# Attention, dense MLP and expert MLP: the stores that fill the token table and clear the output wait until the partial sums and all chunks of x have been read back

## The chip, the cores and the metric

One core of a Trainium2 chip runs the whole program in one launch. The metric is the device time of that launch in microseconds; lower is better. The kernel before took 1200.53 us as the median of three runs (1197.09 to 1201.72).

## What is computed

Three layers follow one another. Attention has 4 batches, 8 heads, 576 tokens and heads of 64 columns, with a decay and a causal mask. Its output x (2304 tokens of 512 columns) goes through a dense MLP of 2048 hidden columns, and that output goes through a layer of 8 experts, of which each token takes two:

```python
decay = cum[:, :, :, None] - cum[:, :, None, :]          # cum: running sum of log f
attn = softmax(where(causal, -1e9, scale * q @ k.T + decay)); x = attn @ v
h = x @ w_in;  y = (h * sigmoid(1.702 * h)) @ w_out       # 512 -> 2048 -> 512
noisy = y @ w_gate + log1p(exp(y @ w_noise)) * noise      # 8 experts, the best two of each token
for e in range(8):                                        # w1: 512 -> 1024, w2: 1024 -> 512
    out[mask] += weight[mask] * (maximum(y[mask] @ w1[e], 0) @ w2[e])
```

All is float32. To keep that accuracy on TensorE, every operand is split into a rounded part (names that end in h) and the rest (names that end in l), and each product is three matmuls: high by high, high by low, low by high.

## The kernel before

The work is written as Python generators, "threads". A class `Planner` runs them on a modelled core while the program is built: a thread yields an operation with its engine and a modelled duration, a buffer token, or an event. The planner emits operations in the order of their modelled start times; among those that could start at the same time the one with the lower priority number goes first. The result is a fixed order of instructions for each engine. On the chip every engine works through its own order, and semaphores keep the data dependences.

All plain transfers are issued by SP into one hardware queue that all 16 DMA engines serve. GpSimd issues only the indirect ones. The planner's model of that queue moves bytes at a fixed rate and lets it run 2.1 us ahead (`DEEP`).

The stages are these. Attention writes x to DRAM in two parts, `x2`, unscaled, with the scale of each token in `rd`. The dense MLP takes x in nine chunks of 256 tokens and its 2048 hidden columns in four quarters. Chunks 0 to 5 (`early_c`) get their first quarter between the products of attention (`filler`, line 1025), and the partial sums of those chunks go out to `yp` (line 1050). When attention has ended, its SBUF is given to `yacc`, the sums of all tokens, and to the remaining chunks of x:

- `yload` (line 1126) reads the six partial sums back, line 1128.
- `xin` (line 1117) reads chunks 6 to 8 (`rest`), and then chunks 0 to 3 once more (`back`); 4 and 5 are still in SBUF (`kept`). One chunk takes four loads of x (line 933) and two of its scales (line 938). DVE or POOL adds the two parts and multiplies by the scale (lines 927 and 928), ACT rounds to `xh` (948), and the rest is `xl` (338 or 339). Each needs one of four staging buffers, `stok`.
- `wprep` (line 341) brings a block of 512 rows or columns of the MLP's weights, also by way of a staging buffer (load: 355). ACT and DVE take the 64-bit words apart (365 to 371), ACT rounds (382), the rest is taken by DVE or POOL (338 or 339).

For each chunk and quarter, line 982 makes h, lines 957 to 962 make the gated gh and gl (ACT, DVE, ACT or POOL, DVE or POOL), and line 1002 adds their products into y. The order is the first quarter of chunks 6 to 8, and then three quarters of all nine, `kept + rest + back` in each. In the last quarter each chunk is routed: its tokens are scattered as rows into the token table `tab` in DRAM, 640 rows for each expert (line 1282). Then each expert reads its rows and adds its results into the output with an accumulating scatter (line 1524).

Before the scatters, every place of the table must hold a padding row and the output must be zero. That is `prefill` (line 1071): 40 stores of 258 KB from the tile `padr` into the table (line 1076), and then 23 stores of 256 KB into the output (line 1079), 63 in all. It has priority 10200, behind the weights of the second and third quarters and the chunks. It waits for `a_done`, the end of attention, and issues a store whenever the modelled queue has nothing with a lower number that is ready.

Of the kernel before, what the change touches and what calls it, by code (L numbers as in the profile page):

```python
# [17 lines left out]
DRAM = bass.MemoryType.DRAM  # L18
# [15 lines left out]


class Tokens:
    """Numbered buffers that threads take and give back."""

    def __init__(self, ids):
        self.free = [(0.0, i) for i in ids]  # L40
# [12 lines left out]


class Planner:
    """Runs generators as threads of a modelled core and emits their instructions in the order of
    the modelled start times, so that every engine's queue holds what can start first.

    A thread yields (engine, us, emit), a Tokens (it is sent the number taken), (Tokens, number) to give
    one back, an Event to wait for, ("set", Event), or ("go", generator, priority)."""  # L60

    LAT = {"PE": 0.2, "ACT": 0.14, "DVE": 0.14, "POOL": 0.14, "DMA": 0.9, "SWQ": 2.2}
    DEEP = 2.1
# [111 lines left out]


def ways(kind, *w):
    """Of the ways to do an operation of a kind, those that it may take."""
    return ("any",) + tuple(x for x in w if x[0] in WAYS.get(kind, ("DVE", "ACT", "POOL")))


# [26 lines left out]

@with_exitstack
def tile_attn_mlp_moe(ctx, tc, q, k, v, f, w_in, w_out, gates, noise, w1, w2, out):  # L210
    """q: [pair, (head d), (tokens 512.., 0..511)], k: [head, d, token], v: [pair, p, i, head, d] of the tokens 128 i + p
    (the last 64: any tokens), w_in and w1: [.., block, p, k, n] of the rows 128 k + p and columns 128 block + n,
    gates: [p, k, (gate, noise)], noise: [p, t, e] of the tokens 128 t + p; w_in and w_out: 64-bit words."""
    nc = tc.nc
    B, H, S = f.shape
    D = k.shape[1]
# [17 lines left out]
    P = Planner()  # L234
# [50 lines left out]
    block = c_([128, CAP // 128], "block")  # L285
# [8 lines left out]

    begun = event()

    # ------------------------------------------------------------------ weights
    watok, wbtok = Tokens(range(4)), Tokens(range(4))
    wplace = {i: wpool for i in range(4)}
    stok = Tokens(range(NST))  # L300
# [12 lines left out]
        return splace.get(i, stg).tile(shape, dt, name=name, tag=f"st{i}")  # L313

    class Weight:
        """A [128, 512] block of weights, split, for `uses` users."""

        def __init__(self, uses, late):
            self.ready, self.uses, self.late = event(), uses, late
# [5 lines left out]


    def rounded(dst, src, n, scale=1.0, kind=""):
        """dst = scale * src, rounded to dst's type."""
        w = onec if scale == 1.0 else eighth
        at = src.base_partition()  # L330
        w = w[at:at + src.shape[0]]
        ones = bass.AP(tensor=w.tensor, offset=w.offset, ap=[list(w.ap[0])] + [[0, x] for x in src.shape[1:]])
        return ways(kind, ("DVE", dve(n / 2), lambda: nc.vector.tensor_scalar(dst, src, scale, None, op0=OP.mult)),
                ("ACT", act(n, True), lambda: nc.scalar.activation(dst, src, AF.Copy, scale=scale)),
                ("POOL", pool1(n), lambda: nc.gpsimd.tensor_tensor(dst, src, ones, op=OP.mult)))
# [3 lines left out]
                ("POOL", pool2(n), lambda: nc.gpsimd.tensor_tensor(dst, a, b, op=OP.subtract)))  # L339

    def wprep(src, wt, pool, letter):
        """A DRAM block of [128, 512] -> a rounded part and the rest; `wd`: of 64-bit words."""
        wd = src.dtype != F32
        n = KD * 128
        yield begun
        if wd:
            ahead = yield pre
        else:
            if wt.late:
                yield placed[letter]  # L350
            sl = yield pool
        st = yield stok
        raw = stage(st, [128, n], src.dtype, "wraw")
        dst = raw.rearrange("p (k n) -> p k n", k=KD) if len(src.shape) == 3 else raw
        yield ("DMA", dma(128 * n * (8 if wd else 4)), lambda: nc.sync.dma_start(dst, src))
        val = raw
        if wd:
            pair = raw.bitcast(F32).rearrange("p (n w) -> p n w", w=2)
            low = raw.bitcast(U32).rearrange("p (n w) -> p n w", w=2)[:, :, 0]
            top, val = pair[:, :, 1], pair[:, :, 0]  # L360
            ut = yield utok
            g = stg.tile([128, n], F32, name="wg_", tag=f"wg{ut}")
            u = stg.tile([128, n], U32, name="wu_", tag=f"wu{ut}")
            gi = g.bitcast(U32)
            yield ("ACT", act(n, True), lambda: nc.scalar.activation(g, top, AF.Abs))
            yield ("DVE", dve(n / 2), lambda: nc.vector.tensor_scalar(g, g, TINY, None, op0=OP.max))
            yield ("DVE", dve(n / 2), lambda: nc.vector.tensor_scalar(
                u, gi, 3, 0x3FFFFFFF, op0=OP.logical_shift_left, op1=OP.bitwise_and))
            yield ("DVE", dve(n), lambda: nc.vector.scalar_tensor_tensor(
                u, top.bitcast(U32), 0xC0000000, u, op0=OP.bitwise_and, op1=OP.bitwise_or))  # L370
            yield ("DVE", dve(n), lambda: nc.vector.scalar_tensor_tensor(
                low, low, 29, u, op0=OP.logical_shift_right, op1=OP.bitwise_or))
            yield (utok, ut)
            sl = yield pool
            yield (pre, ahead)
        if not wt.late:
            nplaced[letter] += 1
            if nplaced[letter] == NQ * FPQ:
                yield ("set", placed[letter])
        wt.pool, wt.slot = pool, sl  # L380
        hi, lo = [wplace[sl].tile([128, n], FR, name=f"w{letter}{x}", tag=f"w{letter}{x}{sl}") for x in "hl"]
        yield ("ACT", act(n, True), lambda: nc.scalar.copy(hi, val))  # L382
        yield subtract(lo, val, hi.bitcast(F32), n, "wl")
        yield (stok, st)
        wt.hi, wt.lo = hi, lo
        yield ("set", wt.ready)

    # ------------------------------------------------------------------ attention
    a_done = event()
    xdone = [event() for _ in range(B)]  # L390
    f_done, c_done = event(), event()
# [2 lines left out]
    def attention(actx):  # L394
        raw, ep, one, sm, xo = [actx.enter_context(tc.tile_pool(name=n, bufs=b)) for n, b in
                                (("a_raw", 1), ("a_e", 1), ("a_one", 1), ("a_sm", 5), ("a_x", 1))]
# [50 lines left out]
        def pair(p):  # L447
            b, hp = divmod(p, PPB)
            base = p * 100.0
            sa = sall[b % 2]  # L450
            # loads
            rw = yield raws
            RQ, RK, vt = [raw.tile(sh, F32, name=f"r{n}", tag=f"r{n}{rw}") for n, sh in
                          (("q", [128, S]), ("k", [128, 2, S]), ("v", [128, 5, 2, D]))]
# [108 lines left out]
            if not p:  # L563
                yield ("set", begun)

            # score tiles
            fronts = [event() for _ in range(5)]
            backs = [event() for _ in range(5)]
            PT = {}
# [2 lines left out]
            def tile_(i):  # L572
# [4 lines left out]
                n = (i + 1) * 128  # L577
# [105 lines left out]
                    if not sleft[b]:  # L683
                        yield ("set", sdone[b])
                yield ("go", ended())
                # transposed probabilities
                if i == 0:
                    PT[2] = yield pt01
                    PT[0] = [one.tile([128, 2, 2, 256], FR, name=f"pt01{x}", tag=f"pt01{x}{PT[2]}") for x in "hl"]
# [133 lines left out]
            P.go(shares(b), b * 100.0 * PPB)  # L823
        return one, init

    # ------------------------------------------------------------------ set-up
    def setup(one, init):
        buf = one.tile([B * H, 5, S], F32, name="buf", tag="pt24h0")
        ft, ones, cum = buf[:, 0], buf[:, 1], buf[:, 2]
# [64 lines left out]
    pad_ok = event()  # L894
    setup(*attention(actx))

    # ------------------------------------------------------------------ dense MLP
    ring = Tokens(range(2))
    gtok = Tokens(range(4))
    gplace = {i: gpool for i in range(4)}  # L900
# [116 lines left out]
            wt = W[letter, fi] = Weight(NCH, False)  # L1017
            P.go(wprep(src, wt, pool, letter), WPRIO + fi if fi < FPQ else 10000 + 90 * (fi // FPQ) - 45 + fi % FPQ)

    # chunks that the first batches fill run between the attention's products  # L1020
    NE_ = B - 1
    early_c = [c for c in range(NCH) if (c + 1) * CH <= NE_ * S]
    ypd = {}
# [43 lines left out]
    for i, c in enumerate(early_c):  # L1067
        ypd[c] = event()
        P.go(filler(c, FP0 + FP1 * i, i and reads[i - 1], reads[i]), FP0 + FP1 * i)

    def prefill():
        yield pad_ok
        yield a_done
        for e in range(E):
            for b in range(CAP // 128):
                yield ("DMA", 0.74, lambda: nc.sync.dma_start(tab[e * RS + b * 128:e * RS + (b + 1) * 128, :], padr))
                yield ("wait", -2.5)
        for b in range(out.shape[0] // 128):
            yield ("DMA", 0.73, lambda: nc.sync.dma_start(out[b * 128:(b + 1) * 128, :], padr[:, 0:DM]))
            yield ("wait", -2.5)  # L1080
# [45 lines left out]
    def yload(c):  # L1126
        yield ypd[c]
        yield ("DMA", 1.46, lambda: nc.sync.dma_start(
            yacc[:, 2 * c:2 * c + 2], yp[c * CH:(c + 1) * CH].rearrange("(t p) d -> p t d", p=128)))
        yield ("set", yin[c])  # L1130

    for i, c in enumerate(rest):
        P.go(xin(c), base - 200 + i)
    for i, c in enumerate(back):
# [2 lines left out]
        P.go(xkept(c), base)  # L1137
    for c in early_c:
        P.go(yload(c), base - 100 + c)

    # ------------------------------------------------------------------ routing
    order = {Q: kept + rest + back for Q in range(NQ)}
    order[0] = rest
    FLOOR = NCH - 4
# [216 lines left out]
            after = turns[Q, c]  # L1361
            n += 1

    # ------------------------------------------------------------------ experts
    NB = CAP // 128
    NBE = EARLY // 128
    EE = list(range(NEE))
# [19 lines left out]
    def group(gi_):  # L1387
# [53 lines left out]
            yield z  # L1441
        if small:
            yield (stok, xs_)
        # products
        if gi_:
            yield mm1_end[gi_ - 1]
        halves = [(0, N)] if N <= 512 else [(0, N // 2), (N // 2, N)]
# [49 lines left out]
    def second(gi_, H_, hev, ids, wab, prio, xet):  # L1497
# [39 lines left out]
        def add(j, b):  # L1537
            wt, (hh, hl, _) = W2[gi_, "b", j], H_[j]
            for n, (a, w) in enumerate(((hh, wt.hi), (hh, wt.lo), (hl, wt.hi))):
                nc.tensor.matmul(ye[b][0], a[:, b * 128:(b + 1) * 128], w, start=(j == 0 and n == 0),  # L1540
                                 stop=(j == FB - 1 and n == 2))
        # the last of the parts go block by block, so that the last group's blocks end one after another
        ends = TJ if gi_ == len(groups) - 1 else 1
        for js in [[j] for j in range(FB - ends)] + [list(range(FB - ends, FB))]:
            for j in js:
# [38 lines left out]
    mctx.close()  # L1584
    body.close()

    # ------------------------------------------------------------------ rows past an expert's slots
    most = nc.values_load(nbi[0:1, E:E + 1], min_val=0, max_val=NOV)
    with tc.If(most > 0), ExitStack() as octx:
        one = octx.enter_context(tc.tile_pool(name="o_one", bufs=1))  # L1590
# [49 lines left out]


def lay(I):
    """The arrays as the kernel takes them; no element changes."""
    import numpy as np
    B, H, S, D = I["q"].shape
    NP = B * H // 2
# [40 lines left out]
```

## Time and profile before

| | |
|---|---|
| runs, median of three | 1200.53 us (1197.09 to 1201.72) |
| profiled execution, span from first to last instruction | 1201.4 us |
| profiled execution, its own time | not listed apart from the three runs above |
| instructions | 18895 |
| PE, weight loads beside it | 1128.1 us (94%), 1000.0 us |
| DVE | 751.1 us (63%) |
| ACT | 529.2 us (44%) |
| POOL | 299.4 us (25%) |
| granted TensorE clock, mean | 0.968 |
| DMA | 167.46 MB, mean 139 GB/s |
| stores of `padr` into the table | 40, issued from 304.0 to 397.8 us |
| stores of `padr` into the output | 23, issued from 398.2 to 415.1 us |

Busy time alone says which engine has the most work, and not what it waits for. The timelines give that: an entry ends, in brackets, with the idle time ahead of it and with what ended it. The granted clock is 1.00 where TensorE has its upper level of 2.4 GHz and 0.50 at the lower one, 1.2 GHz; values between are a mix over the stretch.

### The profile page before, as it was taken

To read this page: it belongs to the slowest core of one execution; us is meant where nothing else is said; L and a number is where in the kernel's file an instruction comes from. 1 tells how busy PE (TensorE), PEld (TensorE's weight loads), DVE (VectorE), ACT (ScalarE), POOL (GpSimd) and SP (SyncE) were. 2 spreads that over 40 slices of the span, in tenths; PEclk is the share of its full clock that TensorE was granted. 3 is DMA by queue.
4 is the path that set the end of the run, shared out by engine and by line. 5 is a ranking of instruction groups with operands and counts; after the bars stand their busy time and mean duration, and the time that the engine had idled before them with its cause. 6 is when DMAs were issued, how large, how long until landed. Compare 5 with 4: busy or idle time off the path is not lost.

```text
span 1201.4 us, 18895 instructions
## 1 busy us (share of the span) xinstructions
PE 1128.1 (94%) x6905; PEld 1000.0 (83%) x6905; DVE 751.1 (63%) x1609; ACT 529.2 (44%) x1251; POOL 299.4 (25%) x316
## 2 busy tenths in 40 slices
PE   7998999999897999999999988999999999999993
PEld 6777888887796998998988877889998989899993
DVE  8999999975558747745777875645434343434410
ACT  4687777674353424433333343544333333333311
POOL 4457654410214001000132343112020202020202
PEclk7998899999898999999999988999999999999997
DMA  8668657619999903101021357676363636262503
GB/s 217 185 189 225 167 153 184 171 66 235 278 280 263 361 2 97 44 1 37 15 96 75 117 160 223 189 191 181 83 152 83 153 78 152 77 158 71 115 1 46
DMA packets 92096, 167.46 MB, mean 139 GB/s; under 512 B 9310, under 2 KB 29534, under 8 KB 91994
## 3 DMA queue, kind: packets, MB, share of 16 engines
q1 hardware_dynamic: 83354, 146.17, 43.1%
q0 software_dynamic: 8640, 20.00, 7.9%
q8 instruction: 56, 0.92, 0.3%
q14 instruction: 46, 0.38, 0.1%
HBM read 112.60 MB, written 49.40 MB: 135 GB/s over the span
## 4 chain that ended last, share of the span: by engine, by line
PE 61%; DVE 15%; DMA 12%; issue 5%; ACT 3%; POOL 2%; SPq 1%; another core or an unknown queue 0%; POOLq 0%; DVEq 0%; ACTq 0%
PE h L1483 15%; PE ye L1540 14%; PE y L1002 12%; PE h L982 12%; PE PT L727 2%; PE O L773 2%; DMA out<-yt,ids 2%; DVE kb L338 1%; DMA xl<-rd 1%; DVE qa L338 1%; DMA xh<-x 1%; POOL out L1524 1%; DVE pt24l L445 1%; DMA xrh<-x 1%; DVE m L585 1%
## 5 line engine op out<-in xcount | busy, mean ns | idle before, releaser
L1467 DVE SCALAR_TENSOR_TENSOR hl<-h,hh 128x320 fp32r<-128x320 f32 (+1 forms) x112 | 56.1, 501 | 213.4 <-ACT hh L1466 212.1
L1466 ACT ACTIVATE hh<-h 128x320 fp32r<-128x320 f32 (+1 forms) x112 | 50.0, 446 | 232.2 <-PE h L1483 232.1
L1524 POOL DMA_INDIRECT out<-yt,ids x36 | 58.5, 1625 | 348.6 <-ACT yt L1519 341.1
L1002 PE MATMUL y<-wbh,gh 128*128 128x512 f32 x288 | 117.6, 408 | 9.2 <-POOL gh L961 4.6
L1002 PE MATMUL y<-wbh,gl 128*128 128x512 f32 x288 | 116.1, 403 | 4.5 <-DVE gl L338 2.7
L957 ACT ACTIVATE t<-h 128x256 f32<-128x256 f32 x144 | 55.4, 385 | 139.1 <-PE h L982 119.8
L1540 PE MATMUL ye<-wbh,hh 128*128 128x512 f32 x288 | 114.4, 397 | 1.3 <-ACT hh L1466 1.3
L1002 PE MATMUL y<-wbl,gh 128*128 128x512 f32 x288 | 115.0, 399 | 0.0
L1540 PE MATMUL ye<-wbh,hl 128*128 128x512 f32 x288 | 113.4, 394 | 0.1
L1540 PE MATMUL ye<-wbl,hh 128*128 128x512 f32 x288 | 113.1, 393 | 0.0
L1483 PE MATMUL h<-xtl,wah 128*128 128x320 f32 (+1 forms) x448 | 86.5, 313 | 0.0
L1483 PE MATMUL h<-xth,wah 128*128 128x320 f32 (+1 forms) x448 | 86.0, 313 | 0.0
L1483 PE MATMUL h<-xth,wal 128*128 128x320 f32 (+1 forms) x448 | 85.7, 313 | 0.0
L589 ACT ACTIVATE e<-S,m 128x384 f32<-128x384 f32 (+3 forms) x128 | 67.3, 530 | 37.2 <-DVE m L585 19.1
L958 DVE SCALAR_TENSOR_TENSOR t<-t,h 128x256 f32<-128x256 f32 x144 | 59.5, 417 | 29.1 <-ACT t L957 26.7
L1483 PEld LDWEIGHTS h<-xth,wah 128*128 128x128 f32 x448 | 73.1, 188 | 4.0
L382 ACT CAST wbh<-wraw 128x512 fp32r<-128x512 f32 x96 | 59.8, 626 | 33.3 <-DMA wraw<-in_w 16.2
L960 ACT CAST gh<-t 128x256 fp32r<-128x256 f32 x126 | 51.0, 407 | 53.1 <-DVE t L958 52.4
L1002 PEld LDWEIGHTS y<-wbh,gl 128*128 128x128 f32 x288 | 55.1, 191 | 21.2 <-DVE gl L338 5.0
L1483 PEld LDWEIGHTS h<-xtl,wah 128*128 128x128 f32 x448 | 72.1, 188 | 0.4
L1483 PEld LDWEIGHTS h<-xth,wal 128*128 128x128 f32 x448 | 71.7, 187 | 0.0
L1002 PEld LDWEIGHTS y<-wbh,gh 128*128 128x128 f32 x288 | 54.9, 191 | 20.1 <-POOL gh L961 5.2
(421 smaller groups left out, 2782.8 us busy)
## 6 DMA issues: line engine op xcount, KB each, us to landing
wraw<-in_w SPq DMA_DIRECT2D x160, 256.0 KB
tab<-padr SPq DMA_DIRECT2D x40, 258.0 KB
rk<-in_k SPq DMA_DIRECT2D x32, 288.0 KB
x<-xo SPq DMA_DIRECT2D x32, 288.0 KB
wraw<-in_w_in SPq DMA_DIRECT2D x16, 512.0 KB
wraw<-in_w_out SPq DMA_DIRECT2D x16, 512.0 KB
xe<-tab SPq DMA_DIRECT2D x6, 1290.0 KB
xa<-x SPq DMA_DIRECT2D x26, 256.0 KB
```

Of the source, the lines that this page charges most:

```text
L382: yield ("ACT", act(n, True), lambda: nc.scalar.copy(hi, val))
L589: yield ("ACT", act(n, extra=2), lambda: nc.scalar.activation(ev[:, h], o, AF.Exp, bias=m[:, h:h + 1], scale=1.0, accum_out=sa[:, 8 * hp + ...
L957: yield ("ACT", act(CH), lambda: nc.scalar.activation(t, h, AF.Tanh, scale=0.851))
L958: yield ("DVE", dve(CH), lambda: nc.vector.scalar_tensor_tensor(t, t, 1.0, h, op0=OP.add, op1=OP.mult))
L960: yield ways("gh", ("ACT", act(CH, True), lambda: nc.scalar.copy(gh, t)), ("POOL", pool1(CH), lambda: nc.gpsimd.tensor_tensor(gh, t, onec. ...
L982: nc.tensor.matmul(h, a[:, kk], z[:, kk], start=(i == 0), stop=(i == len(ops) - 1))
L1002: nc.tensor.matmul(y, a[:, t * 128:(t + 1) * 128], b, start=(fl == 0 and n == 0), stop=(fl == FPQ - 1 and n == 2))
L1466: yield ("ACT", act(c1 - c0), lambda: nc.scalar.activation(hh[:, c0:c1], ps, AF.Relu))
L1467: yield ("DVE", dve(c1 - c0), lambda: stt(hl[:, c0:c1], ps, 0.0, hh[:, c0:c1].bitcast(F32), op0=OP.max, op1=OP.subtract))
L1483: nc.tensor.matmul(ps, a[:, kk], z[:, kk, c0:c1], start=(i == 0), stop=(i == len(ops) - 1))
L1524: st = nc.gpsimd.indirect_dma_start(out=out, out_offset=bass.IndirectOffsetOnAxis(ap=ids[:, b:b + 1], axis=0), in_=yt, in_offset=None, com ...
L1540: nc.tensor.matmul(ye[b][0], a[:, b * 128:(b + 1) * 128], w, start=(j == 0 and n == 0), stop=(j == FB - 1 and n == 2))
```

## The change

`prefill` waits for a new event, `fill_go`, in place of `a_done`. A new thread, `filling`, sets that event once the partial sums of chunks 0 to 5 have been read back (`yin`) and the chunks 0 to 3 of x have been read back and converted (`ready`). Chunks 6 to 8 aren't named in it; their loads have lower priority numbers than those of chunks 0 to 3. The events exist in the planner alone: they set the place of the 63 stores in SP's order, and no semaphore is added to the stores. The stores themselves, their sizes, their priority and their order among themselves stay.

```diff
+    fill_go = event()
+
     def prefill():
         yield pad_ok
-        yield a_done
+        yield fill_go
         for e in range(E):
             for b in range(CAP // 128):
                 yield ("DMA", 0.74, lambda: nc.sync.dma_start(tab[e * RS + b * 128:e * RS + (b + 1) * 128, :], padr))
...
+    def filling():
+        for c in early_c:
+            yield yin[c]
+        for c in back:
+            yield xgo[c]
+            yield X[c].ready
+        yield ("set", fill_go)
+
...
     for c in early_c:
         P.go(yload(c), base - 100 + c)
-
-    # ------------------------------------------------------------------ routing
+    P.go(filling(), base)
```

The rest of the diff takes out comments and docstrings.

## Rows read from the trace of the kernel before

**Rows 1.** The page: busy time by engine; busy tenths of DMA in 40 slices.
```profile
PE 1128.1 (94%) x6905; PEld 1000.0 (83%) x6905; DVE 751.1 (63%) x1609; ACT 529.2 (44%) x1251; POOL 299.4 (25%) x316
...
DMA  8668657619999903101021357676363636262503
```

**Rows 2.** Table by stretch: length, busy (instructions) by engine, granted clock, DMA share, GB/s.
```profile
310.00:320.00 10.00, 5.81 (x22) 4.37 (x21) 5.01 (x7) 2.53 (x5) 3.79 (x4) 0.73 1.09 278
...
350.00:360.00 10.00, 10.00 (x64) 8.89 (x63) 5.03 (x12) 4.64 (x10) 0.00 (x0) 1.00 1.10 248
360.00:370.00 10.00, 5.35 (x26) 3.80 (x25) 7.88 (x12) 3.08 (x10) 3.51 (x2) 0.79 1.11 258
370.00:380.00 10.00, 10.00 (x59) 9.16 (x59) 9.63 (x10) 4.04 (x8) 5.66 (x3) 0.87 1.06 271
380.00:390.00 10.00, 7.49 (x37) 5.30 (x37) 9.46 (x16) 4.15 (x9) 5.21 (x4) 1.00 0.80 254
...
420.00:455.00 35.00, 35.00 (x225) 31.47 (x224) 15.01 (x31) 9.54 (x24) 0.00 (x0) 1.00 0.01 3
```

**Rows 3.** SP's issues in order of time: start, us, line, out<-in, count.
```profile
303.99 0.36 SPq L1076 DMA_DIRECT2D tab<-padr  x1
...
334.32 13.09 SPq L1076 DMA_DIRECT2D tab<-padr  x12
...
349.79 0.58 SPq L933 DMA_DIRECT2D xa<-x  x1
...
368.37 1.74 SPq L938 DMA_DIRECT2D xl<-rd  x2
...
398.24 17.35 SPq L1079 DMA_DIRECT2D out<-padr  x23
```

**Rows 4.** PE's timeline, 355 to 395: start, us, line, shapes, count, [idle before].
```profile
360.70 0.62 PE L982 MATMUL h<-xrl,wah 128*128 128x256 f32 x4
361.16 0.62 PE L982 MATMUL h<-xrh,wal 128*128 128x256 f32 x4
364.87 0.50 PE L1002 MATMUL y<-wbh,gh 128*128 128x512 f32 x1 [3.10 <-ACT gh L960]
...
368.74 0.80 PE L1002 MATMUL y<-wbh,gl 128*128 128x512 f32 x1 [1.47 <-DVE gl L338]
...
372.69 0.39 PE L1002 MATMUL y<-wbh,gl 128*128 128x512 f32 x1
...
381.57 0.40 PE L1002 MATMUL y<-wbl,gh 128*128 128x512 f32 x1
...
388.36 0.50 PE L1002 MATMUL y<-wbh,gl 128*128 128x512 f32 x1 [0.80 <-DVE gl L338]
```

**Rows 5.** DVE's timeline, 290 to 425, in the same form.
```profile
356.48 0.43 DVE L366 TENSOR_SCALAR wg__4338<-wg__4338 128x512 f32<-128x512 f32 x1 [3.92 <-ACT wg__4338 L365]
...
362.82 1.23 DVE L927 TENSOR_TENSOR xa<-xa,xh 128x1024 f32<-128x1024 f32 x1 [2.12 <-issue]
...
366.11 2.58 DVE L338 TENSOR_TENSOR gl<-t,gh 128x256 fp32r<-128x256 f32 x1
...
385.08 1.22 DVE L338 TENSOR_TENSOR xl<-xa,xh 128x1024 fp32r<-128x1024 f32 x1
```

**Rows 6.** The chain that ended last, 335 to 395: start, us, what.
```profile
347.62 8.13 DMA wraw<-in_w_in
```

**Rows 7.** Timelines of SP and ACT from 455: a weight load and its first use.
```profile
460.01 0.34 SPq L355 DMA_DIRECT2D wraw<-in_w_out  x1
...
465.25 0.66 ACT L365 ACTIVATE wg__5561<-wraw 128x512 f32<-128x512 f32 x1 [1.62 <-DMA wraw<-in_w_out]
```

**Rows 8.** POOL's timeline, 290 to 425.
```profile
365.59 2.82 POOL L928 TENSOR_TENSOR xa<-xa,xl 128x1024 f32<-128x1024 f32 x1
...
378.41 3.17 POOL L928 TENSOR_TENSOR xa<-xa,xl 128x1024 f32<-128x1024 f32 x1 [4.20 <-DMA xl<-rd]
```

**Rows 9.** The scatters into the table: duration in ns, first and last start.
```profile
L1282 POOL DMA_INDIRECT tab<-pay,si x36: 957/963/1323, 598.3 to 734.8; - x36
```

## The prediction

> **What bounds the kernel now.** I read the page first, then the forty slices, then a table of busy time by stretch, then the order of issue on SP beside the timelines of DVE, POOL and PE in the stretch that the change touches. The page says that TensorE is the bound: busy 94% of the span, VectorE 63%, ScalarE 44% [rows 1]. An edit in the DMA queue counts only where TensorE has no next operand. The slices, 30 us each, show where to look: around 270 to 420 us the DMA engines are full (the run of nines) and right after it the queue is empty (the digits 0 and 1) [rows 1], between 420 and 455 at a share of 0.01 [rows 2].
>
> The table by stretch splits the crowded part in two. In 310 to 320 PE is busy 5.81 of 10 us, and that is before the stores matter: one of the 63 has been issued by then, at 303.99 [rows 2, 3]. From 320 to 360 PE has no gap (the last ten of these 40 us are shown) although DMA is over 1.0. Then come 360:370 (5.35 busy, clock 0.79) and 380:390 (7.49) [rows 2]. So the target is 360 to 390 us.
>
> How much is lost there? At full pace a group of four 256-column matmuls starts 0.46 us after the last (360.70, 361.16); a 512-column matmul is half of that, 0.23. After the group at 361.16 the next matmul should start at 361.62; it starts at 364.87, and PE is back on full pace at 372.69 [rows 4]. In these 11.07 us it does 8 matmuls of 512 columns and three groups of four, at full pace 8 x 0.23 + 3 x 0.46 = 3.2 us: 7.8 us lost. That is the idle 3.10 and 1.47 us printed in the rows and some 3 us of low clock. From 381.57 to 388.36 it does 7 of the one and three groups of the other, 3.0 us of work in 6.79: 3.8 us lost, in waits of at most 0.80 us with the clock at 1.00 [rows 2, 4]. Together 11.6 us lie within reach of this change, about 1% of the span.
>
> **The path of the first loss.** PE at 364.87 waits for gh on ACT, that for t on DVE, and DVE takes its queue in order: right before t stands the first addition of an x chunk, started at 362.82 after 2.12 us of idleness, because the chunk had not landed [rows 5]. Its loads begin at 349.79, 13.0 us earlier; ahead of them in the queue are 12 token-table stores, issued in one run of 13.09 us from 334.32, and two weight loads [rows 3]. The first of these weight loads took 8.13 us from 347.62 [rows 6], and for it DVE stood idle 3.92 us before 356.48 [rows 5]. So DVE loses 3.92 + 2.12 = 6.0 us to the DMA just before it becomes overfull (9.63 and 9.46 of 10 us busy from 370 to 390) [rows 2].
>
> **The change part by part.**
>
> *Stores taken out of the way.* The 63 stores keep their size and number. 20 of them are issued before the last scale rows of an x chunk at 368.37 (303.99 is the first, the 12 at 334.32 the longest run) and would stand behind instead. The price of one: 23 stores of the output, with hardly anything between them, take SP 17.35 us, 0.75 us each [rows 3]. So the 12 are 9.1 us of queue ahead of the weight and the x chunk.
>
> *First loss.* A weight load with the queue nearly to itself, issued at 460.01, is used on ACT at 465.25: 5.2 us [rows 7]. The one of 347.62 is then there at 352.9 instead of 355.75, and DVE is 2.9 us ahead: it reaches the x addition at about 357.8 instead of 360.70. The x chunk: at best 13.0 - 9.1 = 3.9 us after 349.79, at worst 13.0 as now. The row nearest to it is that weight, which keeps 5.2 of its 8.13 us, 0.64; 0.64 x 13.0 = 8.3, so it lands at 358.1. The addition ends at 359.4, before PE has finished h at 361.6, so gh is in time: the idle 3.10 us go, and the low clock behind them. That the clock goes with them rests on two rows: after 3.10 us of idleness the granted clock fell, after waits of up to 0.80 us at 381 to 388 it stayed at 1.00 [rows 2, 4]. Bounds of this part: 2.1 us (only DVE's last wait goes) to 7.8; taken 3.1 + 2.9 = 6.0, which leaves the 1.47 us and some lag.
>
> *Second loss.* POOL's multiplication at 378.41 waited 4.20 us for the scale rows of its chunk [rows 8]; the gh and gl that PE lacks from 381 on are queued behind it on POOL. These chunks follow one another, each behind a staging buffer that an earlier one frees, so an earlier first chunk moves the next ones. But DVE is nearly full there with its own work. Between 0 and 3.8 us; no row is nearer to one end, so half, 1.9.
>
> *Where the stores go.* The new thread emits no instruction: it holds the stores back in the planner's order, so on the chip they stand on SP behind the last x loads and wait for nothing but the queue. What is queued behind them is weight loads alone. 63 x 0.75 = 47.5 us: started at 372, after the last x load, they end at 419; started at 386, when the last chunk has been converted (the subtraction at 385.08 [rows 5]), at 434. The next load in the queue is due at 460.01 [rows 7], the first scatter into the table at 598.3 [rows 9]. The cover is the empty queue after 420 [rows 2]; without it see the slower rival. The weight loads that now come among the stores had stores among them before and serve a quarter that begins after 455: nothing.
>
> *The order itself.* The planner orders every engine by modelled times, so a lighter modelled DMA can also swap operations between DVE and POOL. No row shows that order. A poor order of these two engines costs 3.8 us at 381 to 388, so I bound it at 3.8 us to either side and take 0.
>
> Sum: 6.0 + 1.9 = 7.9 us less. The profiled execution has a span of 1201.4 us; its own time is not listed apart from the three runs, whose longest is 1201.72, so at most 0.3 us lies around it. The median is 1200.53, 0.9 below the span. From the median, 1200.5 - 7.9 = 1192.6; I say 1192.5.
>
> **The rivals.**
>
> *A. DVE and POOL hold one another up, and that stays.* DVE's gl at 366.11 took 2.58 us beside POOL's 2.82 us multiplication at 365.59 [rows 5, 8], and PE's 1.47 us wait at 368.74 is for that gl [rows 4]. If this and not the queue sets the pace, that wait, the low clock around it and the second loss remain; only 3.1 us and perhaps 1 us of clock go: 1196.5. For it: DVE is full from 370 to 390. Against: the first wait, the longest, has no POOL work in it. The Trainium skill has the rule (SBUF — State Buffer, Who interferes with whom): VectorE and GpSimd share a port pair as an exclusive lock, so a VectorE instruction with two SBUF inputs and a GpSimd one that reads SBUF do not overlap; one waits the other out. The 2.58 us agree with it, as gl ends with POOL's instruction; by the rule alone the time would be this rival's.
>
> *B. The x loads are late by their own size.* Up to 320 they stall PE with one store among them (5.81 of 10 us) [rows 2, 3]. If the later ones, now closer together, just queue behind one another, the same wait forms again for a later chunk: about 1200, within the 3.8 us of reordering. Against: from 320 to 360 no x chunk is late for PE. That the stores would go out early all the same, the change not doing what it says, is counted here; the gate waits for every chunk that is read back, so I see no way to it.
>
> *C. Slower: the stores meet the next quarter's weights.* If the planner holds the block back so far that it starts after 460 - 47.5 = 412.5 us, it runs into the eight weight loads that begin at 460.01. Such a load behind stores took 8.1 us instead of 5.2 [rows 6, 7]; four staging buffers make two rounds of it, 2 x 2.9 = 6 us, and some 2 us of low clock as after the wait at 361: 1208. For it: the gate waits for the conversion of the last chunk, not just its loads. Against: that was at about 386 before, and it would have to come 26 us later with less in its way.
>
> **How the numbers follow.** Forecast 0.55, its own range 1186 to 1196; A 0.20; B 0.12; C 0.13. A difference of 0.5% (6 us) is about what a measurement of this kernel can tell from none, so faster is below 1194.5. Of the forecast 0.47 lies there and 0.08 above; A and three quarters of B (0.09) are no change; C and the rest of B (0.03) are slower: 0.47, 0.37, 0.16. The range starts at 1185 (all 11.6 us and the reordering's 3.8) and ends at 1206 (B with the worst order and a little more), which leaves out most of C.
>
> **What would show it.** In the profile after: no store on SP before the last scale rows of an x chunk; the stretch at 360 with PE over 9 of 10 us busy and the clock near 1.00 (step one right); DVE's idle 3.92 us under 1.5; the stretch at 380 above 8.5 (step two half right); DMA full until 415 to 435 and empty before the third quarter's weights; the same work after 455, about 8 us earlier. Wrong: a PE wait of 3 us for an x chunk between 360 and 400 (B), DVE operations of 2.5 us with PE behind them (A), stores still running when the next weights are due (C), or losses in the routing after 600 us, for which this argument has no row.

## The result: slower by 0.6%, where a gain of 0.7% was forecast

The changed kernel took 1206.01 us (median of six runs, 1203.89 to 1208.92) against 1200.64 us of the kernel before (1196.60 to 1201.72) on the same chip. The ratio is 1.0058 with a 95% interval of 1.0037 to 1.0078: 5.4 us slower by the medians, where 8 us faster was predicted. The profiled execution took 1206.62 us with a span of 1204.8 us.

The page of the changed kernel, against [rows 1]: the engines do the same work. In the DMA slices, of some 30 us each, the run of five nines is now broken by a 6 and a 7 (331 to 391 us), and the queue stays busy one slice longer.

```profile
PE 1127.0 (94%) x6905; PEld 997.8 (83%) x6905; DVE 751.1 (62%) x1611; ACT 528.4 (44%) x1249; POOL 296.8 (25%) x316
...
DMA  8668657619967962100012357665353636362503
```

The table by stretch, against [rows 2] (columns as there):

```profile
310.00:320.00 10.00, 4.81 (x15) 3.20 (x13) 5.04 (x7) 1.91 (x4) 3.06 (x3) 0.66 1.00 250
...
330.00:340.00 10.00, 9.55 (x65) 8.60 (x63) 2.61 (x6) 2.30 (x5) 0.00 (x0) 1.00 1.08 228
340.00:350.00 10.00, 6.64 (x22) 4.50 (x23) 9.03 (x14) 3.98 (x8) 3.22 (x2) 0.83 0.10 23
...
360.00:370.00 10.00, 9.23 (x59) 7.94 (x59) 8.46 (x16) 6.00 (x13) 2.47 (x2) 1.00 0.69 172
370.00:380.00 10.00, 7.14 (x36) 5.66 (x35) 7.31 (x8) 2.71 (x6) 4.25 (x2) 1.00 1.12 234
380.00:390.00 10.00, 6.84 (x45) 5.71 (x44) 9.42 (x18) 5.03 (x11) 3.93 (x2) 0.91 0.52 171
390.00:400.00 10.00, 10.00 (x50) 8.79 (x49) 6.51 (x13) 2.92 (x6) 0.85 (x1) 0.75 1.05 354
```

The predicted improvement is there: 360:370 has PE busy 9.23 us at full clock, where it had 5.35 at 0.79. But 340:350, without a gap before, now has 6.64 busy at a clock of 0.83, 370:380 fell from 10.00 to 7.14, and 380:390 is no better. The moments at which both traces have done the same amount of matmul work, counted in columns from the start, tell how late PE is: within 1 us of nothing up to 330, +7.4 us at 360, +1.2 at 370, +6.2 from 390 on. An event with a record of its own agrees: the first weight load of a later quarter, issued at 460.01 [rows 7], now is at 466.20, 6.2 us later. At the end of this one execution the span is 3.4 us longer. So one stall went (-6.2), two came (+7.3, +4.9).

SP's issues in order of time, against [rows 3]:

```profile
331.44 1.25 SPq L938 DMA_DIRECT2D xl<-rd  x2
350.27 0.57 SPq L933 DMA_DIRECT2D xa<-x  x1
...
354.65 0.35 SPq L355 DMA_DIRECT2D wraw<-in_w_in  x1
...
387.22 2.42 SPq L1078 DMA_DIRECT2D tab<-padr  x4
...
400.34 20.32 SPq L1078 DMA_DIRECT2D tab<-padr  x25
420.79 15.89 SPq L1081 DMA_DIRECT2D out<-padr  x23
...
466.20 0.34 SPq L355 DMA_DIRECT2D wraw<-in_w_out  x1
```

No store stands before 387.22, and the last is out at 436.7, thirty us ahead of the next weights. The new thing is the hole: SP issues nothing from 332.7 to 350.27. SP's waits name the reason for the load at 350.27: 11.2 of these 17.6 us are on DVE's `xl` (L338). Chunk 1 of x stands in the order ahead of the weights, and it takes a staging buffer that chunk 0 still holds. From 340 to 350 the queue is nearly empty (DMA share 0.10), and the weights behind it go out at 354.65 instead of 347.62 [rows 6].

What holds chunk 0 itself is seen in the timelines of DVE, ACT, POOL and PE from 330 to 350:

```profile
332.02 0.69 DVE L371 SCALAR_TENSOR_TENSOR wraw<-wraw,wu__4099 128x512 uint32<-128x512 uint32 x1
340.44 1.22 DVE L927 TENSOR_TENSOR xa<-xa,xh 128x1024 f32<-128x1024 f32 x1 [7.72 <-DMA xl<-rd]
341.58 0.74 DVE L958 SCALAR_TENSOR_TENSOR t<-t,h 128x256 f32<-128x256 f32 x2
...
342.02 0.66 ACT L365 ACTIVATE wg__4148<-wraw 128x512 f32<-128x512 f32 x1 [4.87 <-DVE t L958]
...
342.13 0.61 POOL L961 TENSOR_TENSOR gh<-t,onec 128x256 fp32r<-128x256 f32 x1 [14.07 <-DVE t L958]
...
342.80 0.50 PE L1002 MATMUL y<-wbh,gh 128*128 128x512 f32 x1 [3.25 <-POOL gh L961]
```

DVE is idle 7.72 us before the first addition of chunk 0, and `t`, which PE needs by way of gh, stands behind it. In the kernel before, POOL did that addition, off DVE's path and at nearly the same time, so the chunk itself landed hardly earlier for the change:

```profile
341.44 2.39 POOL L928 TENSOR_TENSOR xa<-xa,xh 128x1024 f32<-128x1024 f32 x1 [1.02 <-DMA xl<-rd]
```

PE's timeline from 368 to 388, against [rows 4], has the second new loss: the casts and rests of the weights that went out late (`wah`, `wbh`, `wbl`), and then a gh again.

```profile
368.05 0.72 PE L982 MATMUL h<-xrh,wah 128*128 128x256 f32 x4 [0.24 <-ACT wah L382]
...
374.67 0.49 PE L1002 MATMUL y<-wbh,gh 128*128 128x512 f32 x1 [1.42 <-ACT wbh L382]
...
376.60 0.50 PE L1002 MATMUL y<-wbl,gh 128*128 128x512 f32 x1 [1.44 <-POOL wbl L339]
...
387.64 0.50 PE L1002 MATMUL y<-wbh,gh 128*128 128x512 f32 x1 [2.59 <-ACT gh L960]
```

### The profile page after: what moved, and what is told of

Read it like the earlier page. It is cut to its first block, busy times and chain, and to the rows that moved or that the text cites. A ratio compares the mean times of both kernels' runs of the same rounds, so it can differ in the third digit from the quotient of the medians.

```text
span 1204.8 us, 18901 instructions
## 1 busy us (share of the span) xinstructions
PE 1127.0 (94%) x6905; PEld 997.8 (83%) x6905; DVE 751.1 (62%) x1611; ACT 528.4 (44%) x1249; POOL 296.8 (25%) x316
## 4 chain that ended last, share of the span: by engine, by line
PE 64%; DVE 14%; DMA 11%; issue 5%; ACT 2%; POOL 2%; SPq 1%; DVEq 0%; POOLq 0%; ACTq 0%
PE h L1494 15%; PE ye L1551 14%; PE y L1002 13%; PE h L982 13%; PE O L773 3%; DMA xl<-rd 2%; PE PT L727 2%; DMA out<-yt,ids 2%; POOL out L1535 1%; DVE kb L338 1%; DVE pt24l L445 1%; DMA wraw<-in_w 1%; DMA xrl<-rd 1%; SPq L933 1%; DVE m L585 1%
## 5 line engine op out<-in xcount | busy, mean ns | idle before, releaser
L727 PE MATMUL PT<-identf,e 128*128 128x128 f32 (+1 forms) x400 | 63.6, 287 | 8.1 <-ACT e L589 5.9
```

Of the source, the lines that this page charges most:

```text
L727: nc.tensor.transpose(ps[0:w.shape[1], o:o + 128], w, identf)
```

## The experiments

The change does two things at once: it moves stores on SP, and it makes the planner write another order for all engines (some 70 places of DVE's order differ). Two theories were to be told apart. The stores theory: their new place costs or gains the time. The order theory: the new order costs it, and under it, that the planner places work by an x load that it takes to be faster than it is (2.9 us for four loads of 256 KB, 360 GB/s, where the chip moves some 230). Each ratio is to the kernel before on the same chip, with its 95% interval. The traces are of one execution each; those of the block kernel (1219.03 us) and of the factor 1.25 (1197.69 us) are of the longest of their runs.

**The old order with late stores, in a block.** The planner counts the stores as before, and the orders of PE, DVE, ACT and POOL are those of the kernel before; only the real stores are kept until the gate opens.

```diff
+    def when_open(put):
+        kept_back.append(put)
+        if fill_go.at is not None:
+            while kept_back:
+                kept_back.pop(0)()
...
-                yield ("DMA", 0.74, lambda: nc.sync.dma_start(tab[e * RS + b * 128:e * RS + (b + 1) * 128, :], padr))
+                yield ("DMA", 0.74, lambda: when_open(put))
```

> The kernel before with every engine's order unchanged: the planner still counts the 63 stores at their old places, but SP gets them only once the last x chunk has been converted in the order, as in the changed kernel. Theory O (the new order of DVE, POOL and the loads is what costs; the stores going later is a gain): the 360 us loss of the kernel before goes, 5 to 8 us faster than before, 1193 to 1196. Theory S (the late stores themselves cost, by what they run beside): as slow as the changed kernel, about 1206.

Measured: 1213.46 us, ratio 1.0101 (1.0084 to 1.0119), slower than both theories had it. Up to 390 us it lost nothing; then came a stall that neither theory had. SP's timeline first, then ACT's and PE's:

```profile
380.05 19.66 SPq L1086 DMA_DIRECT2D tab<-padr  x27
400.40 0.34 SPq L355 DMA_DIRECT2D wraw<-in_w_out  x1
...
408.12 0.66 ACT L365 ACTIVATE wg__4812<-wraw 128x512 f32<-128x512 f32 x1 [11.44 <-DMA wraw<-in_w_out]
...
409.13 0.79 PE L1002 MATMUL y<-wbh,gh 128*128 128x512 f32 x1 [10.14 <-ACT gh L960]
```

Twenty-seven stores in one run stood ahead of a weight load that was at 386.36 before. That weight serves a quarter that begins much later, but its first step on ACT is queued ahead of a gh that PE needs at once. This kernel says nothing on the stores' place as the change has it, only what a block of them can cost.

**The old order with late stores, spread.** As above, but the stores that stand ahead of the gate go to the very end and the others keep their places. On the chip these are 26: the 20 ahead of the last x load, and 6 more among the weights after it.

```diff
+    def when_open(put):
+        sofar[0] += 1
+        if fill_go.at is None:
+            kept_back.append(put)
+        else:
+            put()
+        while sofar[0] == 63 and kept_back:
+            kept_back.pop(0)()
```

> The kernel before with every engine's order unchanged. The 20 stores that stood ahead of the last x load are left out there and issued after the last store of the output; all other stores keep their places among the weight loads, so there is no block of 27 in front of one. Theory O (the late stores are a gain of a few us, the new order is the loss): 1196 to 1199. Theory S (late stores cost by themselves): above 1204. If the block of 27 is what made the earlier kernel with late stores slow (ACT waited 11.4 us there for a weight load issued behind it), its 13 us vanish here.

Measured: 1199.46 us, ratio 0.9978 (0.9959 to 0.9998). Its table by stretch, and PE's one wait between 361 and 370:

```profile
360.00:370.00 10.00, 7.86 (x50) 6.86 (x49) 8.67 (x11) 4.29 (x10) 4.85 (x3) 0.87 1.12 228
...
380.00:390.00 10.00, 6.57 (x28) 4.43 (x29) 9.34 (x16) 4.02 (x9) 4.90 (x4) 1.00 0.55 156
```

```profile
367.26 0.70 PE L1002 MATMUL y<-wbh,gl 128*128 128x512 f32 x1 [2.08 <-DVE gl L338]
```

The wait of 3.10 us is gone, the one for gl stays, and 380:390 is poorer than before (7.49 of 10 us) with the queue nearly half empty. This is close to the predicted edit with no other engine's order moved: worth 0.2%, 2 to 3 us (1.8 by the medians, 2.6 by the ratio), and not 7.9.

**The new order with early stores.** The orders of the changed kernel, with 20 stores put back among the x loads and the reads of the partial sums.

```diff
+            if X.get(c) is x and c in (0, 1):
+                stores((12, 1)[c])
...
+            stores({4: 1, 5: 4, 6: 2}.get(seen["y"], 0))
...
+            yield ("DMA", 0.74, lambda: stores(1) if seen["left"] > 0 else None)
```

> The changed kernel with every engine's order unchanged, but 20 of the stores are put back among the loads at the places that they had before. Theory O: the new order keeps its cost and the old queue cost comes on top: 1206 plus up to 8, slower than the changed kernel, 1208 to 1214. Theory S: back at the time of the kernel before, about 1200.5.

Measured: 1207.80 us, ratio 1.0062 (1.0041 to 1.0083), against 1.0058 of the changed kernel. So with the new order the time is the same with these stores early or late, and with the old order late stores, if spread, gain 0.2%. The order carries the whole loss: some 7 us with the stores early, and 0.8% or 9.6 us between the two kernels that have them late (1.0058 against 0.9978).

**Which part of the order: one addition back on POOL.** The changed kernel with one instruction moved, chunk 0's first addition.

```diff
-            return ways("xa", ("DVE", dve(n), lambda: nc.vector.tensor_tensor(xa, xa, z, op=op)),
+            one = nc.gpsimd if c == 0 and op == OP.add and X.get(0) is x else nc.vector
+            return ways("xa", ("DVE", dve(n), lambda: one.tensor_tensor(xa, xa, z, op=op)),
```

> The changed kernel with one instruction moved: the first addition of x chunk 0 runs on POOL instead of DVE, as in the kernel before; nothing else in any order differs. Theory O: DVE no longer waits 7.7 us for that chunk with t queued behind it, PE's idle time at 339 to 346 goes, 5 to 6.5 us faster than the changed kernel, 1199.5 to 1201. If the late weight loads are the real limit behind it, the gain is given back at 370 to 390 and the time stays at 1204 to 1206.

Measured: 1207.59 us, ratio 1.0059 (1.0035 to 1.0082): no gain, and no theory had forecast this time. The stall only changed hands, as the timelines of POOL, ACT and PE show:

```profile
345.79 2.34 POOL L928 TENSOR_TENSOR xa<-xa,xh 128x1024 f32<-128x1024 f32 x1 [12.20 <-DMA xl<-rd]
...
347.91 0.67 ACT L365 ACTIVATE wg__4148<-wraw 128x512 f32<-128x512 f32 x1 [5.24 <-DMA wraw<-in_w_out]
...
348.76 0.80 PE L1003 MATMUL y<-wbh,gh 128*128 128x512 f32 x1 [3.69 <-POOL gh L962]
```

POOL has a gh behind that addition, and ACT waits for a weight that went out behind the same x loads. On either engine, something that PE needs stands behind the first use of the late load.

**A nudge of the planner.** The kernel before with the modelled price of a table store at 0.70 instead of 0.74: nothing real changes but the order (some 60 places on DVE).

```diff
-                yield ("DMA", 0.74, lambda: nc.sync.dma_start(tab[e * RS + b * 128:e * RS + (b + 1) * 128, :], padr))
+                yield ("DMA", 0.70, lambda: nc.sync.dma_start(tab[e * RS + b * 128:e * RS + (b + 1) * 128, :], padr))
```

> The kernel before with one modelled number nudged: the planner takes a table store at 0.70 us instead of 0.74. No store is held back; the order of DVE changes in about as many places as in the changed kernel. Theory O says nothing of its sign, it only says that a new order by itself may move some us either way. If it stays within 2 us of before, a new order as such is not worth 7 us and the changed order has a particular fault; if it moves by 4 us or more, orders of this kernel differ by that much at a nudge.

Measured: 1202.83 us, ratio 1.0014 (0.9995 to 1.0034). This nudge is worth between nothing and 4 us (2.4 by the medians, between the two bounds that were set); the changed kernel's loss is larger, and one nudge doesn't show how far orders of this kernel can lie apart.

**The right pace, in the changed kernel.** The planner's price for loading a chunk of x after attention is multiplied by 1.54, which makes it some 233 GB/s. The edit is in the model alone.

```diff
+        k = 1.54 if X.get(c) is x else 1.0
-        yield ("DMA", 2.9, load, 4)
-        yield ("wait", -3.0)
-        yield ("go", one_op(("DMA", 1.46, rload, 2), rok))
-        yield ("wait", 3.0)
+        yield ("DMA", 2.9 * k, load, 4)
+        yield ("wait", -3.0 * k)
+        yield ("go", one_op(("DMA", 1.46 * k, rload, 2), rok))
+        yield ("wait", 3.0 * k)
```

> The changed kernel with one figure of the planner corrected after attention: an x chunk's loads are taken at 1.54 times the time, about 233 GB/s as the trace has it for them, instead of 360. Theory P (the planner believes that a chunk lands earlier than it does, puts its additions and the weight conversions ahead of gh and gl, and takes the chunk's next load ahead of the second quarter's weights; the stores had hidden that by making the modelled queue slower): the idle time at 339 to 346 and the weight waits at 368 to 377 shrink, 1195 to 1201. Rival N (any new order is a throw of some us): anywhere from 1198 to 1208, with the 339 us stall still there or moved.

Measured: 1189.41 us (1184.85 to 1191.79), ratio 0.9899 (0.9875 to 0.9923), faster than even theory P had it. Table by stretch, then a line of DVE's timeline and one of PE's:

```profile
310.00:320.00 10.00, 10.00 (x68) 9.15 (x67) 5.05 (x8) 4.61 (x10) 3.43 (x4) 1.00 1.03 239
...
330.00:340.00 10.00, 10.00 (x63) 8.87 (x63) 8.96 (x16) 5.65 (x12) 2.21 (x2) 1.00 0.74 183
340.00:350.00 10.00, 9.04 (x55) 7.69 (x55) 9.38 (x17) 5.55 (x13) 3.51 (x2) 1.00 0.31 80
...
380.00:390.00 10.00, 9.73 (x60) 8.05 (x59) 8.93 (x18) 4.73 (x11) 2.17 (x2) 1.00 0.95 304
```

```profile
334.94 1.21 DVE L927 TENSOR_TENSOR xa<-xa,xh 128x1024 f32<-128x1024 f32 x1
...
361.73 0.50 PE L1003 MATMUL y<-wbh,gh 128*128 128x512 f32 x1 [2.53 <-ACT wbh L382]
```

DVE does other work until the chunk is there (8.96 us busy from 330 to 340, where the changed kernel has 2.61) and starts the addition without a wait. From 300 to 360 PE has no wait over 0.96 us: the stall of 340 to 350 is gone, and so is the one of 310 to 320 that both kernels had. There DVE's timelines show the cause plainly, first of the kernel before, then of this one:

```profile
311.95 1.22 DVE L927 TENSOR_TENSOR xa<-xa,xl 128x1024 f32<-128x1024 f32 x1 [1.70 <-DMA xl<-rd]
313.10 0.74 DVE L958 SCALAR_TENSOR_TENSOR t<-t,h 128x256 f32<-128x256 f32 x2
```

```profile
309.83 0.42 DVE L959 SCALAR_TENSOR_TENSOR t<-t,h 128x256 f32<-128x256 f32 x1
...
312.71 1.23 DVE L927 TENSOR_TENSOR xa<-xa,xl 128x1024 f32<-128x1024 f32 x1 [1.56 <-DMA xl<-rd]
```

The scale rows land no earlier and DVE waits for them as long, but `t` now stands ahead of that wait and not behind it. Counted in columns, 6.8 of the 11.5 us by which this kernel leads the one before from 400 on come between 310 and 320, and 3.1 after 330. At 361 to 363 PE still waits 2.53 us for `wbh` and 1.09 for `wbl`, parts of a weight; from there to 400 it has no wait over 0.3 us. After 330 the edit also moves loads: the weight that the changed kernel issues behind chunk 1 of x (354.65) now goes ahead of it, at 337.11 against 345.07. How much is the weight's and how much the first uses' isn't separated there. A later quarter's first weight is issued at 448.53, 11.5 us ahead of the kernel before.

**The right pace, in the kernel before.** The same edit without the change.

> The kernel before with the same corrected pace, stores at their old gate. Theory P: little or a small gain, 1197 to 1201, as its order was already late enough. If it is as fast as the changed kernel with the corrected pace, holding the stores back is worth nothing; if it is slower by 2 to 5 us, that is what holding them back is worth.

Measured: 1189.92 us, ratio 0.9902 (0.9880 to 0.9924). With x loads priced right, the gate is worth nothing that can be measured (0.5 us between the medians), and its loss is gone. The next weight is at 449.08, 0.6 us after that of the changed kernel with the right pace.

**Other paces.** The factor 1.25, and 2.0, in the changed kernel.

> The changed kernel with the modelled time of an x chunk's loads after attention at 1.25 times instead of 1.54. Theory P: part of the way, 1190 to 1200, with part of the stalls at 311, 339 and 361 left. Rival N (any order is a throw): no relation to the factor, 1198 to 1208 as likely as anything lower.

> The same with a factor of 2.0, slower than the trace has it. Theory P: no stall on an x chunk comes back, as its users are only placed later still; near the corrected pace, 1188 to 1196, some us lost if chunks then come too late in the order. Rival N: 1198 to 1208.

Measured: 1192.64 us, ratio 0.9917 (0.9895 to 0.9939), and 1189.17 us, ratio 0.9895 (0.9870 to 0.9921). Factors 1.0, 1.25, 1.54 and 2.0 give 1206.0, 1192.6, 1189.4 and 1189.2 us: most of the gain comes with the first step, and a load priced too dear costs no time here, though PE then waits 4.70 us for `wah` at 358.43. Four paced kernels, each with another order, lie within 4 us of one another and 9 to 13 us under the kernel before. That is what a consumer placed too early would do; lucky orders are not a likely account of all four. At 1.25 short waits remain at 313 to 318 us (1.19, 0.69, 1.10) and at 364 to 368 (1.55 twice).

**One more staging buffer**, in the changed kernel and together with the factor 1.54, to see whether the hole on SP is the loss.

```diff
-NSX = 0
+NSX = 1
```

> The changed kernel with a fifth staging buffer after attention. Theory P, second part (x chunk 1 took the staging buffer that the second quarter's weights had in the kernel before, so SP stood 11.2 us and the queue ran empty at 340 to 350): the gap of the queue and the weight waits at 368 to 377 shrink, 3 to 5 us faster than the changed kernel, 1201 to 1203, with the stall at 339 to 346 still there. If staging is not the gate: no change, 1206, or a throw of the new order.

> The changed kernel with the corrected pace of 1.54 and a fifth staging buffer. If staging still limits once the order is right, 2 to 4 us below the corrected pace alone, 1185 to 1188; if nothing in 290 to 400 waits any more, the same 1189, within the few us of a new order.

Measured: 1201.72 us, ratio 0.9998 (0.9979 to 1.0017), and 1191.87 us, ratio 0.9916 (0.9895 to 0.9938). The stall at 344 remains (2.16 us), as theory P had said. The buffer wins 4 us (by the medians) to 7 us (by the ratios) back with the wrong pace and nothing with the right one. As it changes the whole order (190 places on DVE, stalls at 300.11, 317.85 and 362.94), it doesn't show how much the buffer's wait alone is worth.

**Three instructions held back.** The changed kernel with DVE's first addition of chunk 0 and its next step of the weight put behind two gl, and ACT's first step of that weight behind one gh; at most four places each.

```diff
+                if c == 0 and op == OP.add and X.get(0) is x:
+                    hold("DVE", put)
...
+        def high():
+            nc.scalar.copy(gh, t)
+            passed("ACT", 1)
...
+            nc.vector.tensor_tensor(gl, t, gh.bitcast(F32), op=OP.subtract)
+            passed("DVE", 2)
```

> The changed kernel with three instructions moved by at most four places and nothing else: DVE's first addition of x chunk 0 and the first DVE step of the next weight go behind the two gl ahead of which they stood, and that weight's first step on ACT goes behind one gh. Theory P says that these three, waiting for transfers with gh and gl queued behind, are the stall at 339 to 346: it goes, and 4 to 6 us of the 7 with it, 1200 to 1202. If the x additions come late by it and the loss forms again at 360 to 390, 1204 to 1206.

Measured: 1205.55 us, ratio 1.0026 (1.0009 to 1.0043). By the ratios some 4 us of the loss come back, with intervals that overlap, and the trace doesn't show where: the stall has moved a step on, as its table by stretch and PE's timeline tell.

```profile
330.00:340.00 10.00, 10.00 (x69) 9.12 (x68) 4.60 (x10) 3.14 (x7) 0.61 (x1) 1.00 1.07 222
340.00:350.00 10.00, 4.98 (x19) 3.62 (x18) 7.80 (x10) 2.96 (x7) 2.36 (x1) 0.77 0.21 38
```

```profile
344.96 0.50 PE L1041 MATMUL y<-wbh,gh 128*128 128x512 f32 x1 [2.93 <-ACT gh L993]
...
347.89 0.79 PE L1041 MATMUL y<-wbh,gl 128*128 128x512 f32 x1 [2.08 <-DVE gl L998]
```

So how the loss divides between the wait at chunk 0 and the late weights behind it stays open. That the loss is the order's is shown by the kernels that hold the order and move the stores; that it goes with the pace, by the paced kernels.

## Why the prediction was wrong

**What bounds the kernel, and the 11.6 us within reach.** Right that PE stood for its operands in those two places. But of the 11.6 us there even the right pace gets some 3; most of its gain, 6.8 us, is the stall of 310 to 320, which the prediction had set aside because the stores don't make it.

**Stores taken out of the way.** Right as a fact on SP: no store before 387.22.

**First loss, 6.0 us.** The mechanism was right and the size wrong. The spread kernel tests it with the order held: its weight is there in time (DVE has no wait where it had 3.92 us), and PE's wait of 3.10 us for gh is gone. SP's line of the chunk's first load, then DVE's and POOL's:

```profile
351.75 0.59 SPq L933 DMA_DIRECT2D xa<-x  x1
...
361.33 1.23 DVE L927 TENSOR_TENSOR xa<-xa,xh 128x1024 f32<-128x1024 f32 x1 [1.67 <-DMA xh<-x]
...
364.63 2.58 DVE L338 TENSOR_TENSOR gl<-t,gh 128x256 fp32r<-128x256 f32 x1
...
364.12 2.81 POOL L928 TENSOR_TENSOR xa<-xa,xl 128x1024 f32<-128x1024 f32 x1
...
378.65 2.63 POOL L928 TENSOR_TENSOR xa<-xa,xl 128x1024 f32<-128x1024 f32 x1 [5.91 <-DMA xl<-rd]
```

The chunk took 9.6 us from its first load to its addition, where 8.3 were taken. (The row of the kernel before names `issue` for DVE's wait there, and not the load; this one names the load.) Then gl again took 2.58 us beside POOL, PE's wait for it grew from 1.47 to 2.08 us, and the clock still fell, to 0.87 in 360:370. Counted in columns, PE is 1.9 us late at 360 in this execution and 1.6 early at 370: 3.5 us gained. The changed kernel makes up 6.2 there, the forecast's own size, but only after a stall of its own that gave the loads that time.

**Second loss, 1.9 us.** Wrong, and it went the other way: 380:390 stayed poor in the old order with late stores, 6.57 of 10 us, and from 370 to 390 PE gives back 1.3 of the 3.5 us. POOL's multiplication for the last chunk starts at 378.65, where it started at 378.41 [rows 8]: the first chunk's earlier addition didn't bring the last one's scale rows. And half of what PE waits for from 382 on in the kernel before is gl from DVE (1.24 us) and not gh from POOL (1.26). For the wait on gl and for the second loss rival A was right, with DVE over nine tenths busy. With the order held, the time is 1199.5, nearer to A's 1196.5 than to the forecast.

**Where the stores go.** Their place was forecast well: 387 to 437, with the queue empty before the next weights at 466.20; rival C didn't happen. But the sentence that weights among the stores cost "nothing" is false in general. The block kernel lost 10.14 us on PE in one wait for a weight that is wanted much later, because ACT takes its queue in order. It didn't hurt in the changed kernel: PE has no wait from 390 to 470, although 48 stores in a row go out ahead of the weight at 436.92. What a block costs depends on what stands behind the weight's first step.

**The order itself, ±3.8 us and taken as 0.** This is the step that failed. The order that the planner writes without the stores costs some 7 us with the stores early (1.0062) and 9.6 us with them late (1.0058 against 0.9978), two to two and a half times the bound that I had put on it. Of the 15 us by ratio between the forecast (7.9 less) and the result (7.0 more), these are 9.6; the rest is the size of the two losses, 2.6 us in place of 7.9. I had read the bound from one place (381 to 388) and had not asked what the stores did inside the model. The stores had made the modelled queue slow, and so hidden that x loads are modelled at 360 GB/s while [rows 2] had the full queue at 248 to 278 GB/s, stores among them. Without stores the planner believes that a chunk lands earlier than it does, and puts its first use ahead of what PE needs next. The modelled times, which the planner gives as it writes the program, bear this out: without the stores chunk 0's loads start 3.7 us earlier in the model (261.00 against 264.68), take 5.9 us in both, and its first addition is placed 4.9 us earlier (266.88 against 271.78). On the chip the loads went out 2.2 us earlier (328.18 against 330.39), took some 12 us, and the addition began 1.0 us earlier (340.44 against 341.44). With the pace put right the loss is gone and the gate is worth nothing.

**The rivals.** B, for which the stall of 310 to 320 was the evidence, named the right kind of loss, x loads late by their own size and the wait formed again at another chunk (chunk 0, at 340), with too small a price (1200); the run lies at the end of the stated range, 1206, which stood for B with the worst order. A describes what is left of the old loss. C's danger, stores ahead of a weight, the block kernel met and the changed one did not.

## What to carry to other kernels

When instructions are ordered by a model, an edit of one queue is an edit of every engine's order, and it can be timed apart: keep the order and move the work, then keep the work and move the order. Price each kind of transfer by the rate that the trace shows for it; one number for x loads that was half as high again as the measured rate cost this kernel 1%, about four times what the edit alone won. An engine that takes its queue in order makes the first step of any prefetch a possible stall of the main path, so the first use of a load that may land late belongs behind the work that is due.

## What the runs showed of the hardware

Loads of x and of its scales moved much slower than stores of about the same 256 KB at the same busy share of the queue: 228 GB/s at a share of 1.12 (360:370 of the spread kernel, where SP issues nothing else) and 354 at 1.05 (390:400 of the changed kernel, stores and two weights). Why wasn't tried. The loads fill 64 partitions each, the stores read 128, and the packets differ: of the loads' 2351 all but one are under 2 KB, in the other stretch 200 of 1771.

POOL held DVE up in a form that I had not looked for. In the changed kernel a one-input DVE step takes 0.43 us alone and 2.60 beside POOL's multiplication, which takes 2.60 as well; DVE's timeline, then POOL's:

```profile
330.83 0.43 DVE L367 TENSOR_SCALAR wu__4099<-wg__4098 128x512 uint32<-128x512 uint32 x1
...
343.73 2.60 DVE L367 TENSOR_SCALAR wu__4149<-wg__4148 128x512 uint32<-128x512 uint32 x1
...
343.44 2.60 POOL L928 TENSOR_TENSOR xa<-xa,xl 128x1024 f32<-128x1024 f32 x1 [0.69 <-DMA xl<-rd]
```

The Trainium skill (SBUF — State Buffer, Who interferes with whom) says that a `tensor_scalar` can run in a mode that takes both port pairs and then locks GpSimd out or is locked out by it for the whole instruction. These two rows agree with it.
